# A new layout for the first three blocks of a convolution and MLP kernel: both token halves in both partition halves, W_in swapped by DMA

## The chip, the cores and the metric

The kernel runs on one core of a Trainium2 chip. The metric is device time in microseconds (us); a kernel is compared with another of the same rounds on the same chip. All times inside a kernel are counted from the start of its profiled span.

## The reference

A depthwise causal convolution with softmaxed weights (8 heads, 7 taps) over x of 8 x 4096 x 192, then an MLP with exact GELU:

```python
w = softmax(weight)                                  # 8 x 7
out[b, s, h, g] = sum_k w[h, k] * x_pad[b, s + k, h, g]
h = out.reshape(32768, 192) @ w_in                   # w_in 192 x 2048
g = 0.5 * h * (1 + erf(h / sqrt(2)))
result = g @ w_out                                   # w_out 2048 x 192
```

## The kernel before

The 32768 tokens are cut in two halves. Partitions 0 to 63 hold channels of the first half, partitions 64 to 127 the same channels of the second half; 192 channels make three pieces p. The tokens of a half are worked through in blocks: four of 256, then thirty of 512. For each block VectorE transposes x, the convolution is made (blocks 0 to 2 on TensorE with diagonal matrices, later ones on VectorE), mm1 multiplies by W_in, ACT applies GELU, and mm2 multiplies by W_out while mm1 of the next block runs.

Both partition halves need all of W_in. To save start-up traffic each half loads only one half of its columns, and TensorE copies the other half across:

```python
def dup(s):                                          # 4 pieces of 256 columns
    ...
    for p in range(NP):
        for hf in range(2):
            ins = t.matmul(DUPB[s][ro, p * FQ : (p + 1) * FQ], idb[r, :],
                           win[r, p * F + s * FQ : p * F + (s + 1) * FQ],
                           tile_position=(64 * hf, 64 - 64 * hf))
    ins.then_inc(S_DUP)

def pconv(n, p):                                     # blocks 0 to 2
    ...
    for k in range(KS - 1, -1, -1):
        for hf in range(2):
            ins = t.matmul(b[r, o : o + w], dg[r, d0 : d0 + 64], xTb[n][r, x0 : x0 + w],
                           start=(k == KS - 1), stop=(k == 0),
                           tile_position=(64 * hf, 64 * hf))
```

The loads. POOL issues W_in in two parts and then `wout` (W_out); SP issues the weight table, half of block 0's x, then, after the first part of W_in has landed, the rest, up to block 3; block 4 follows once block 1 has been transposed. ACT issues the other halves of blocks 0 and 1 at once.

```python
# POOL
win_in(0, FQ, S_WIN[0])
...                                                  # masks
win_in(FQ, FH, S_WIN[1])
g.dma_start(wout..., woutt...).then_inc(S_WOUT, 16)
for n in range(NB):
    halo(n)
# SP
load(sp, 0, (0, 1)); sp.wait_ge(S_WIN[0], 32)
load(sp, 1, (0, 1)); load(sp, 2); load(sp, 3)
for n in range(1, NB):
    if n + 3 < NB:
        load(sp, n + 3)                              # waits until the buffer is transposed
    store(sp, n - 1)
```

The first mm2 stands in block 1 and waits for `wout`:

```python
if n == 1 and i == i0:                               # i0 = 2
    t.wait_ge(S_WOUT, 16)
for un in todo[a0:a1]:
    mm2(n - 1, *un)
```

## Time and profile before

| | before |
|---|---|
| time, medians over the sessions | 700.4 to 702.2 us |
| span of the profiled run | 698.3 us |
| TensorE busy | 99% |
| first mm1 / first mm2 | 12.70 / 28.74 us |
| block 2 / block 5 starts on TensorE | 38.93 / 77.36 us |
| `wout` issued / landed | 5.66 / about 25.6 us |

From about 80 us on both kernels have the same rhythm, 0.66 us of mm1 and 0.66 us of mm2 in turn. A difference in time is therefore a difference in the start of block 5. The lines that carry this are shown in the prediction.

### The profile page before, as it was taken

The numbers are of one execution on the slowest core, as the hardware profiler recorded it, in microseconds if no ns is written. First come the engines' busy times: TensorE is split into PE (matmuls) and PEld (weight loads), VectorE is DVE, ScalarE is ACT, GpSimd is POOL, SyncE is SP. The second block draws the span as 40 slices with busy tenths as digits, with TensorE's granted clock in tenths as the row PEclk, the third lists the DMA queues.
The fourth block names the chain that finished last, engine by engine and source line by source line (L and its number), as shares of the span: only waits on it lengthen the run. The fifth ranks groups of instructions, "written<-read, shape, count | busy, mean of one in ns | idle before, by whom it ended". The sixth has DMA issues, their size and how long they took to land.

```text
span 698.3 us, 25401 instructions
## 1 busy us (share of the span) xinstructions
PE 689.0 (99%) x11625; PEld 528.7 (76%) x11625; DVE 551.5 (79%) x908; ACT 529.0 (76%) x524; POOL 39.5 (6%) x87
## 2 busy tenths in 40 slices
PE   8999999999999999999999999999999999999998
PEld 4797677777777777777777777777777777777777
DVE  3599978898888898888898888898888898888811
ACT  4577877777777777777777777777777777777771
POOL 4100000000000000000000000000000000000000
PEclk9999999999999999999999999999999999999999
DMA  9758533555533555533455533455533455521013
GB/s 202 157 131 194 125 75 86 120 136 137 121 88 84 119 136 138 121 86 87 118 137 137 121 93 82 116 137 136 129 87 82 114 137 136 124 60 24 24 48 92
DMA packets 22667, 78.15 MB, mean 112 GB/s; under 512 B 6945, under 2 KB 10785, under 8 KB 18721
## 3 DMA queue, kind: packets, MB, share of 16 engines
q1 hardware_dynamic: 18832, 73.80, 44.4%
q0 software_dynamic: 2896, 1.57, 1.6%
q8 instruction: 91, 1.49, 0.9%
q10 hardware_dynamic: 832, 1.16, 0.6%
q14 instruction: 16, 0.12, 0.1%
HBM read 52.92 MB, written 25.17 MB: 112 GB/s over the span
## 4 chain that ended last, share of the span: by engine, by line
PE 96%; DVE 3%; issue 1%; POOL 0%; ACT 0%; POOLq 0%; DVEq 0%
PE ob L650 48%; PE hp L616 46%; DVE acc L403 1%; PE ob L579 1%; PE hp L523 1%; DVE xT L373 0%; DVE xc L403 0%; DVE acc L396 0%; PE ob L529 0%; POOL win L229 0%; DVE osb L412 0%; ACT gT L509 0%; DVE win L344 0%; PE ob L551 0%; POOL sel L237 0%
## 5 line engine op out<-in xcount | busy, mean ns | idle before, releaser
L509 ACT ACTIVATE gT<-hp 128x1024 bf16<-128x1024 f32 x512 | 523.5, 1024 | 148.5 <-PE hp L616 148.5
L650 PEld LDWEIGHTS ob<-wout,gT 64*128 64x128 bf16 x8192 | 367.7, 94 | 100.0 <-PE ob L650 0.6
L650 PE MATMUL ob<-wout,gT 64*128 64x192 bf16 x8192 | 427.9, 243 | 0.1
L616 PE MATMUL hp<-xc,win 64*128 64x512 bf16 (+1 forms) x3264 | 422.9, 363 | 3.6 <-DVE xc L403 1.6
L403 DVE SCALAR_TENSOR_TENSOR acc<-xT,wcol,acc 128x512 f32<-128x512 f32 (+1 forms) x465 | 311.1, 733 | 0.0
L616 PEld LDWEIGHTS hp<-xc,win 64*128 64x128 bf16 x3264 | 165.0, 94 | 57.3 <-ACT gT L509 4.3
L412 DVE COPY osb<-ob 128x384 f32<-128x384 f32 x128 | 70.4, 550 | 125.1 <-PE ob L650 125.0
L403 DVE SCALAR_TENSOR_TENSOR xc<-xT,wcol,acc 128x512 bf16<-128x512 f32 (+1 forms) x93 | 63.4, 734 | 0.0
L373 DVE STREAM_TRANSPOSE xT<-xin 128x512 f32<-128x512 f32 (+1 forms) x102 | 61.2, 649 | 0.0
L396 DVE TENSOR_SCALAR acc<-xT,wcol 128x512 f32<-128x512 f32 (+1 forms) x93 | 54.1, 633 | 1.1
L302 POOL COPY xT<-xT 128x558 f32<-128x558 f32 x31 | 20.2, 652 | 590.1 <-DVE xT L373 590.1
L285 POOL COPY xT<-xT 128x18 f32<-128x18 f32 x28 | 11.1, 398 | 0.0
L579 PE MATMUL ob<-xTb,dg 64*64 64x256 bf16 x126 | 9.1, 291 | 0.3 <-DVE xTb L351 0.3
L579 PEld LDWEIGHTS ob<-xTb,dg 64*64 64x64 bf16 x126 | 6.8, 116 | 2.8 <-issue 1.1
L359 DVE CAST xc<-ob 128x256 bf16<-128x256 f32 x6 | 2.5, 422 | 6.8 <-PE ob L579 6.8
L523 PE MATMUL hp<-warm 128*128 128x512 bf16 x13 | 5.9, 629 | 1.3 <-DVE warm L313 1.3
L344 DVE CAST win<-ob 128x768 bf16<-128x768 f32 x3 | 2.9, 952 | 3.6 <-PE ob L551 3.6
L523 PEld LDWEIGHTS hp<-warm 128*128 128x128 bf16 x13 | 1.6, 137 | 3.8 <-issue 2.5
L296 POOL CAST xTb<-xT 128x186 bf16<-128x186 f32 x9 | 3.4, 384 | 14.6 <-DVE xT L373 14.6
L488 ACT ACTIVATE xc<-ob 128x256 bf16<-128x256 f32 x3 | 1.2, 384 | 3.2 <-PE ob L579 3.2
L344 DVE CAST win<-hp 128x768 bf16<-128x768 f32 x1 | 1.0, 958 | 3.2 <-PE hp L551 3.2
L480 ACT ACTIVATE xTb<-xT 128x256 bf16<-128x256 f32 x3 | 1.1, 417 | 2.8 <-DVE xT L373 2.8
(34 smaller groups left out, 21.4 us busy)
## 6 DMA issues: line engine op xcount, KB each, us to landing
xin<-in_x_dram SPq DMA_DIRECT2D x120, 380.0 KB, 6.7
out_dram<-osb SPq DMA_DIRECT2D x116, 192.0 KB, 3.1
xin<-in_x_dram SPq DMA_DIRECT2D x12, 188.0 KB, 7.3
out_dram<-osb SPq DMA_DIRECT2D x40, 48.0 KB, 1.8
wout<-in_moe_w_out_dram POOLq DMA_DIRECT2D x1, 768.0 KB, 19.9
xin<-in_x_dram ACTq DMA_DIRECT2D x4, 188.0 KB, 5.4
win<-in_moe_w_in_dram POOLq DMA_DIRECT2D x2, 288.0 KB, 6.3
out_dram<-osb ACTq DMA_DIRECT2D x8, 48.0 KB, 2.0
```

The costliest lines, as they stand in the source:

```text
L285: g.tensor_copy(dst, ap(xT[(n - 1) % 2], WS[n - 1] + 31, [[NP * XW, 128], [XW, NP], [32, HB]],),).then_inc(S_HALO)
L302: g.tensor_copy(ap(t, 1, [[NP * tw, 128], [tw, NP], [32, HB], [1, 31]]), ap(t, WS[n], [[NP * tw, 128], [tw, NP], [32, HB], [1, 31]]),).the ...
L344: v.tensor_copy(ap(win, FH + s * FQ, [[NP * F, 128], [F, NP], [1, FQ]]), ap(DUPB[s], 0, [[1024, 128], [FQ, NP], [1, FQ]]),).then_inc(S_DUPE)
L373: v.transpose(ap(xT[n % 2], p * XW + HL, [[NP * XW, 128], [1, w]]), ap(xin[n % NX], 64 * p, [[TB // 32 * D, 128], [D, w // 32], [1, 32]],) ...
L396: ins = v.tensor_scalar(a, src, wk, None, ALU.mult)
L403: ins = v.scalar_tensor_tensor(dst, src, wk, a, op0=ALU.mult, op1=ALU.add)
L412: v.tensor_copy(ap(osb[m % 2], g * C, [[8 * C, 128], [4 * C, 2], [1, C]]), ap(ob[(G0[m] + g) % 2], 0, [[1024, 128], [512, 2], [1, C]]),).t ...
L509: a.activation(out=ap(gT[n % 2], i * c * 2 * w, dst), in_=ap(hp[u % 2], 0, src), func=AF.Gelu,).then_inc(S_GELU)
L523: t.matmul(hp[1][:, 0:512], warm[:, 0:128], warm[:, :])
L579: ins = t.matmul(b[r, o : o + w], dg[r, d0 : d0 + 64], xTb[n][r, x0 : x0 + w], start=(k == KS - 1), stop=(k == 0), tile_position=(64 * hf, ...
L616: ins = t.matmul(hp[u % 2][:, hf * TB + cc * w : hf * TB + cc * w + w], win[r, p * F + wcols(hf, f0) : p * F + wcols(hf, f0) + 128], xc[n ...
L650: ins = t.matmul(ob[gg % 2][:, 512 * sub : 512 * sub + C], gT[m % 2][r, c0 : c0 + 128], wout[r, CH[i] * C : (CH[i] + 1) * C], start=(ph == ...
```

## The change

Its intent: in blocks 0 to 2 a 64-row partition half works only with the half of W_in that it holds, on the tokens of both halves. The convolution then has to deliver every token to both partition halves, which it does by using four 64x64 tiles per tap instead of two. No copying on TensorE and no casts on VectorE are needed; the other half of W_in comes later by a DMA inside SBUF, the swap, for block 3. The softmax is made on all 128 partitions, from a weight table broadcast at load. `wout` is issued later, so that block 1's x comes first.

```diff
-    wsb 8x7, sel 8 x 384, three fp32 matmuls to spread the weights ...
+    wsb 128 x 56, mask msk, softmax on 128 partitions ...
-            def dup(s): ... 4 x 6 matmuls, 4 casts on VectorE
 # convolution, blocks 0 to 2
-                        b[r, o : o + w], ... tile_position=(64 * hf, 64 * hf)
+                    for cf in range(2):
+                        CONVB[n][p][64 * cf : 64 * cf + 64, 512 * hf : 512 * hf + w], ...
+                        tile_position=(64 * hf, 64 * cf)
 # mm1, blocks 0 to 2
+                if n < ND:
+                    for p in range(NP):
+                        for hf in range(2):
+                            t.matmul(hp[u % 2][:, hf * TB : (hf + 1) * TB],
+                                     win[r, p * F + 128 * i : p * F + 128 * i + 128],
+                                     xc[n % 2][r, p * TB : (p + 1) * TB], ...)
 # POOL
-            win_in(FQ, FH, S_WIN[1]); wout issued here
+            win_in(FQ, 2 * FQ, S_WIN[1]); win_in(2 * FQ, FH, S_WIN[2])
+            halo(0)
+            g.wait_ge(S_XIN[1], 64)          # block 1's x has landed
+            wout issued here
 # ACT
+            a.wait_ge(S_WSB, 16)
             load(a, 0, (2, 3))
-            load(a, 1, (2, 3))
 # SP
-            load(sp, 1, (0, 1))
+            load(sp, 1)
             load(sp, 2)
             load(sp, 3)
+            for i in range(3): sp.wait_ge(S_WIN[i], 32)
+            for hf in range(2):
+                sp.dma_start(win of half hf, columns FH.., from win of half 1 - hf, columns 0..FH)
+                  .then_inc(S_WIN[3], 16)
 # VectorE: reads of mm2 results of block 0, position (block, instruction)
-            late = {(0, 0): (3, 4), (0, 1): (3, 14), ...
+            late = {(0, 0): (3, 10), (0, 1): (3, 18), ...
```
(cut: index arithmetic, the softmax instructions, the convolution taps spread between the mm1 units, PSUM buffers and semaphore counts)

More of the change, by code (lines that the diff above doesn't have):

```diff
@@ L62, in bass_lightweight_conv__then__act_gelu_exact_kernel @@
     G0 = [sum(NG[:n]) for n in range(NB + 1)]
-    CH = []
-    for s in range(4):
-        CH += [2 * s, 2 * s + 1, NF // 2 + 2 * s, NF // 2 + 2 * s + 1]
+    CH = [NF // 2 * h + i for i in range(NF // 2) for h in range(2)]
     PLAIN = [NCH[n] > 1 or n == NB - 1 for n in range(NB)]
@@ L91, in bass_lightweight_conv__then__act_gelu_exact_kernel @@
         wout = sbt("wout", [128, NF * C], BF16)
-        wsb = sbt("wsb", [H, KS], F32)
-        wmx = sbt("wmx", [H, 1], F32)
-        wsm = sbt("wsm", [H, 1], F32)
-        wrc = sbt("wrc", [H, 1], F32)
-        wex = sbt("wex", [H, KS], F32)
-        wnm = sbt("wnm", [H, KS], F32)
-        sel = sbt("sel", [H, NP * 128], F32)
+        wsb = sbt("wsb", [128, H * KS], F32)
+        wmx = sbt("wmx", [128, H], F32)
+        wsm = sbt("wsm", [128, H], F32)
+        wrc = sbt("wrc", [128, H], F32)
+        wex = sbt("wex", [128, H * KS], F32)
+        wnm = sbt("wnm", [128, H * KS], F32)
+        msk = sbt("msk", [128, NP * H], F32)
+        wpr = sbt("wpr", [128, NP * KS * H], F32)
         wcol = sbt("wcol", [128, NP * KS], F32)
@@ L114, in bass_lightweight_conv__then__act_gelu_exact_kernel @@
         S_WSB = sem("S_WSB")
-        S_WIN = [sem("S_WIN%d" % i) for i in range(2)]
+        S_WIN = [sem("S_WIN%d" % i) for i in range(4)]
         S_WOUT = sem("S_WOUT")
@@ L118, in bass_lightweight_conv__then__act_gelu_exact_kernel @@
         S_OUT = [sem("S_OUT%d" % i) for i in range(2)]
-        S_MSET = sem("S_MSET")
-        S_SEL = sem("S_SEL")
+        S_MSK = sem("S_MSK")
         S_IDN = sem("S_IDN")
-        S_PEP = sem("S_PEP")
         S_WARM = sem("S_WARM")
@@ L130, in bass_lightweight_conv__then__act_gelu_exact_kernel @@
         S_PCE = sem("S_PCE")
-        S_DUP = sem("S_DUP")
-        S_DUPE = sem("S_DUPE")
         S_HALO = sem("S_HALO")
@@ L142, in bass_lightweight_conv__then__act_gelu_exact_kernel, with pce @@
         block = es.enter_context(nc.Block())
-        DUPB = [hp[0], ob[1], ob[0], ob[1]]
-        CONVB = [
-            [(ob[0], 0), (ob[0], 512), (ob[1], 0)],
-            [(ob[0], 0), (ob[0], 512), (ob[1], 0)],
-            [(ob[1], 0), (ob[1], 512), (ob[1], 256)],
-        ]
+        CONVB = [[ob[0], ob[1], hp[1]], [ob[0], ob[1], ob[0]], [ob[1], ob[1], ob[1]]]
+        def pce(n, p):
+            return NP * n + p + 1 + (min(p + 1, NP) if n == 0 else NP)
         NCV = NP * KS
@@ L234, in _ @@
             win_in(0, FQ, S_WIN[0])
-            g.wait_ge(S_MSET, 2)
-            pat = [[64, NP], [0, 2], [1, 64]]
-            g.affine_select(
-                out=sel[:, :],
-                in_=sel[:, :],
-                compare_op=ALU.is_ge,
-                fill=0.0,
-                base=0,
-                pattern=pat,
-                channel_multiplier=-GRP,
-            ).then_inc(S_SEL)
-            g.wait_ge(S_SEL, 1)
-            g.affine_select(
-                out=sel[:, :],
-                in_=sel[:, :],
-                compare_op=ALU.is_ge,
-                fill=0.0,
-                base=GRP - 1,
-                pattern=[[-a, b] for a, b in pat],
-                channel_multiplier=GRP,
-            ).then_inc(S_SEL)
+            g.memset(msk[:, :], 1.0).then_inc(S_MSK)
+            g.memset(idb[:, :], 1.0).then_inc(S_MSK)
+            g.wait_ge(S_MSK, 2)
+            for hf in range(2):
+                m = msk[64 * hf : 64 * hf + 64, :]
+                g.affine_select(
+                    out=m,
+                    in_=m,
+                    compare_op=ALU.is_ge,
+                    fill=0.0,
+                    base=0,
+                    pattern=[[64, NP], [-GRP, H]],
+                    channel_multiplier=1,
+                ).then_inc(S_MSK)
+            g.wait_ge(S_MSK, 4)
+            for hf in range(2):
+                m = msk[64 * hf : 64 * hf + 64, :]
+                g.affine_select(
+                    out=m,
+                    in_=m,
+                    compare_op=ALU.is_ge,
+                    fill=0.0,
+                    base=GRP - 1,
+                    pattern=[[-64, NP], [GRP, H]],
+                    channel_multiplier=-1,
+                ).then_inc(S_MSK)
             for hf in range(2):
@@ L266, in _ @@
                 ).then_inc(S_IDN)
-            win_in(FQ, FH, S_WIN[1])
-            g.dma_start(
-                ap(wout, 0, [[NF * C, 128], [C, NF], [1, C]]),
-                ap(woutt, 0, [[C, 128], [128 * C, NF], [1, C]]),
-            ).then_inc(S_WOUT, 16)
+            win_in(FQ, 2 * FQ, S_WIN[1])
+            win_in(2 * FQ, FH, S_WIN[2])
             def halo(n):
@@ L278, in halo @@
                     g.wait_ge(S_CV, cvd(n - 2))
-                elif n >= 2:
-                    g.wait_ge(S_PCE, NP * (n - 1))
+                elif n >= ND:
+                    g.wait_ge(S_PCE, pce(n - 2, NP - 1))
                 if OFF[n] % SEQ == 0:
@@ L307, in _ @@
             g.wait_ge(S_IDN, 2)
-            for n in range(NB):
+            halo(0)
+            g.wait_ge(S_XIN[1], 64)
+            g.dma_start(
+                ap(wout, 0, [[NF * C, 128], [C, NF], [1, C]]),
+                ap(woutt, 0, [[C, 128], [128 * C, NF], [1, C]]),
+            ).then_inc(S_WOUT, 16)
+            for n in range(1, NB):
                 halo(n)
@@ L313, in _ @@
             v.memset(warm[:, :], 0.0).then_inc(S_WARM)
-            v.memset(sel[:, :], 1.0).then_inc(S_MSET)
-            v.memset(idb[:, :], 1.0).then_inc(S_MSET)
+            hk = [[H * KS, 128], [KS, H], [1, KS]]
             v.wait_ge(S_WSB, 16)
             v.tensor_reduce(
-                wmx[:, :], wsb[:, :], mybir.AxisListType.X, ALU.max, negate=True
+                wmx[:, :], ap(wsb, 0, hk), mybir.AxisListType.X, ALU.max, negate=True
+            ).then_inc(S_PRO)
+            v.wait_ge(S_PRO, 1)
+            v.tensor_tensor(
+                ap(wex, 0, hk), ap(wsb, 0, hk), ap(wmx, 0, [[H, 128], [1, H], [0, KS]]), ALU.add
             ).then_inc(S_PRO)
             v.wait_ge(S_ACTP, 2)
+            v.tensor_reduce(
+                wsm[:, :], ap(wnm, 0, hk), mybir.AxisListType.X, ALU.add
+            ).then_inc(S_PRO)
+            v.wait_ge(S_PRO, 3)
             v.tensor_scalar(wsm[:, :], wsm[:, :], 1e-9, None, ALU.add).then_inc(S_PRO)
-            v.wait_ge(S_PRO, 2)
+            v.wait_ge(S_PRO, 4)
             v.reciprocal(wrc[:, :], wsm[:, :]).then_inc(S_PRO)
-            v.wait_ge(S_PRO, 3)
-            v.tensor_scalar(
-                wnm[:, :], wex[:, :], wrc[:, 0:1], None, ALU.mult
+            v.wait_ge(S_PRO, 5)
+            v.tensor_tensor(
+                ap(wex, 0, hk), ap(wnm, 0, hk), ap(wrc, 0, [[H, 128], [1, H], [0, KS]]), ALU.mult
             ).then_inc(S_PRO)
-            v.wait_ge(S_PEP, 1)
-            v.tensor_copy(wcol[:, :], ob[0][:, 0 : NP * KS]).then_inc(S_PRO)
-            v.wait_ge(S_PRO, 5)
+            v.wait_ge(S_PRO, 6)
+            v.wait_ge(S_MSK, 6)
+            v.tensor_tensor(
+                ap(wpr, 0, [[NP * KS * H, 128], [KS * H, NP], [H, KS], [1, H]]),
+                ap(wex, 0, [[H * KS, 128], [0, NP], [1, KS], [KS, H]]),
+                ap(msk, 0, [[NP * H, 128], [H, NP], [0, KS], [1, H]]),
+                ALU.mult,
+            ).then_inc(S_PRO)
+            v.wait_ge(S_PRO, 7)
+            v.tensor_reduce(
+                wcol[:, :],
+                ap(wpr, 0, [[NP * KS * H, 128], [H, NP * KS], [1, H]]),
+                mybir.AxisListType.X,
+                ALU.add,
+            ).then_inc(S_PRO)
+            v.wait_ge(S_PRO, 8)
             v.wait_ge(S_IDN, 2)
@@ L339, in diag @@
                 ).then_inc(S_DG)
-            def dup_out(s):
-                v.wait_ge(S_DUP, s + 1)
-                v.tensor_copy(
-                    ap(win, FH + s * FQ, [[NP * F, 128], [F, NP], [1, FQ]]),
-                    ap(DUPB[s], 0, [[1024, 128], [FQ, NP], [1, FQ]]),
-                ).then_inc(S_DUPE)
             def cast(n, p):
@@ L357, in conv_out @@
                 v.wait_ge(S_PC, NP * n + p + 1)
-                b, o = CONVB[n][p]
+                hs = [1] if n == 0 else [0, 1]
                 v.tensor_copy(
-                    xc[n % 2][:, p * TB : p * TB + WS[n]], ap(b, o, [[1024, 128], [1, WS[n]]])
+                    ap(
+                        xc[n % 2],
+                        p * TB + 128 * hs[0],
+                        [[NP * TB, 128], [128, len(hs)], [256, 2], [1, 128]],
+                    ),
+                    ap(
+                        CONVB[n][p],
+                        512 * hs[0],
+                        [[1024, 128], [512, len(hs)], [128, 2], [1, 128]],
+                    ),
                 ).then_inc(S_PCE)
@@ L369, in trans @@
                     elif n >= 2:
-                        v.wait_ge(S_PCE, NP * (n - 1))
+                        v.wait_ge(S_PCE, pce(n - 2, NP - 1))
                     if n >= 1:
@@ L427, in _ @@
             diag(0)
-            diag(1)
             for p in range(NP):
                 trans(0, p)
+            diag(1)
             diag(2)
-            for q in range(3):
-                dup_out(q)
+            for p in range(NP):
+                conv_out(0, p)
             for n in range(1, ND):
@@ L438, in _ @@
                     cast(n, p)
-                if n == 1:
-                    dup_out(3)
-                for p in range(NP):
-                    conv_out(n, p)
-            late = {(0, 0): (3, 4), (0, 1): (3, 14), (1, 0): (4, 1), (1, 1): (4, 9)}
+                if n < ND - 1:
+                    for p in range(NP):
+                        conv_out(n, p)
+            late = {(0, 0): (3, 10), (0, 1): (3, 18), (1, 0): (4, 1), (1, 1): (4, 9)}
             late.update({(2, 0): (4, 16), (2, 1): (4, 23), (3, 0): (5, 14), (3, 1): (6, 1)})
@@ L455, in _ @@
                 for o, op in enumerate(ops0):
+                    if b == ND and o in (2, 5, 8):
+                        conv_out(ND - 1, o // 3)
                     while order and late[order[0]] <= (b, o):
@@ L465, in _ @@
             a.activation(out=hot[:, 0:1], in_=warm[0:1, 0:1], func=AF.Exp).then_inc(S_ACTP)
+            a.wait_ge(S_WSB, 16)
             load(a, 0, (2, 3))
             a.wait_ge(S_ACTP, 1)
-            a.wait_ge(S_PRO, 1)
-            a.activation(
-                out=wex[:, :],
-                in_=wsb[:, :],
-                func=AF.Exp,
-                bias=wmx[:, 0:1],
-                accum_out=wsm[:, 0:1],
-            ).then_inc(S_ACTP)
+            a.wait_ge(S_PRO, 2)
+            a.activation(out=wnm[:, :], in_=wex[:, :], func=AF.Exp).then_inc(S_ACTP)
             a.activation(out=hot[:, 1:2], in_=warm[0:1, 0:1], func=AF.Gelu).then_inc(S_HOT)
-            load(a, 1, (2, 3))
             for p in range(NP):
@@ L486, in _ @@
                 a.wait_ge(S_PC, p + 1)
-                b, o = CONVB[0][p]
                 a.activation(
-                    out=xc[0][:, p * TB : p * TB + WS[0]],
-                    in_=ap(b, o, [[1024, 128], [1, WS[0]]]),
+                    out=ap(xc[0], p * TB, [[NP * TB, 128], [256, 2], [1, 128]]),
+                    in_=ap(CONVB[0][p], 0, [[1024, 128], [128, 2], [1, 128]]),
                     func=AF.Copy,
@@ L500, in _ @@
                         a.wait_ge(S_MM2, G0[n - 1])
-                    if not PLAIN[n]:
+                    if n < ND:
+                        src = [[2 * TB, 128], [1, 2 * TB]]
+                        dst = [[NF * 2 * TB, 128], [1, 2 * TB]]
+                    elif not PLAIN[n]:
                         src = [[2 * TB, 128], [w // 4, 8], [32, w // 128], [1, 32]]
@@ L520, in _ @@
             t.wait_ge(S_WARM, 1)
-            def spin(k):
-                for i in range(k):
-                    t.matmul(hp[1][:, 0:512], warm[:, 0:128], warm[:, :])
-            spin(5)
-            t.wait_ge(S_SEL, 2)
-            t.wait_ge(S_PRO, 4)
-            for p in range(NP):
-                ins = t.matmul(
-                    ob[0][:, p * KS : (p + 1) * KS],
-                    sel[:, p * 128 : (p + 1) * 128],
-                    wnm[:, :],
-                )
-            ins.then_inc(S_PEP)
@@ L535, in _ @@
-            spin(8)
-            def dup(s):
-                if s == 0:
-                    t.wait_ge(S_IDN, 2)
-                    t.wait_ge(S_WIN[0], 32)
-                elif s == 1:
-                    t.wait_ge(S_WIN[1], 32)
-                    t.wait_ge(S_PCE, NP)
-                elif s == 3:
-                    t.wait_ge(S_DUPE, 2)
-                for p in range(NP):
-                    for hf in range(2):
-                        r = slice(64 * hf, 64 * hf + 64)
-                        ro = slice(64 - 64 * hf, 128 - 64 * hf)
-                        ins = t.matmul(
-                            DUPB[s][ro, p * FQ : (p + 1) * FQ],
-                            idb[r, :],
-                            win[r, p * F + s * FQ : p * F + (s + 1) * FQ],
-                            tile_position=(64 * hf, 64 - 64 * hf),
-                        )
-                ins.then_inc(S_DUP)
@@ L559, in pconv @@
-            def pconv(n, p):
-                w = WS[n]
-                b, o = CONVB[n][p]
-                t.wait_ge(S_CAST, NP * n + p + 1)
-                t.wait_ge(S_HALO, HC[n] + 2 + p)
-                if n == 0:
-                    t.wait_ge(S_DG, p + 1)
-                elif n == 1 and p == 0:
-                    t.wait_ge(S_DUPE, 3)
-                elif n == 1 and p == 2:
-                    t.wait_ge(S_DUPE, 4)
-                elif n == 2 and p == 0:
-                    t.wait_ge(S_PCE, 2 * NP)
-                elif n == 2 and p == 2:
-                    t.wait_ge(S_PCE, 2 * NP + 1)
-                for k in range(KS - 1, -1, -1):
-                    for hf in range(2):
-                        r = slice(64 * hf, 64 * hf + 64)
-                        d0 = (p * KS + k) * 64
-                        x0 = p * XB + 32 * k
-                        ins = t.matmul(
-                            b[r, o : o + w],
+            for i in range(16):
+                t.matmul(hp[0][:, 0:512], warm[:, 0:128], warm[:, :])
@@ new lines, in pconv @@
+            def pconv(n, p, k):
+                w = WS[n]
+                if k == KS - 1:
+                    t.wait_ge(S_CAST, NP * n + p + 1)
+                    if n == 0:
+                        t.wait_ge(S_DG, p + 1)
+                    elif n == 1 and p == 2:
+                        t.wait_ge(S_PCE, pce(1, 0))
+                    elif n == 2:
+                        t.wait_ge(S_PCE, pce(2, p) - 1)
+                if k == KS - 2:
+                    t.wait_ge(S_HALO, HC[n] + 2 + p)
+                for hf in range(2):
+                    r = slice(64 * hf, 64 * hf + 64)
+                    d0 = (p * KS + k) * 64
+                    x0 = p * XB + 32 * k
+                    for cf in range(2):
+                        ins = t.matmul(
+                            CONVB[n][p][64 * cf : 64 * cf + 64, 512 * hf : 512 * hf + w],
@@ L584, in pconv @@
                             stop=(k == 0),
-                            tile_position=(64 * hf, 64 * hf),
+                            tile_position=(64 * hf, 64 * cf),
                         )
-                ins.then_inc(S_PC)
-            pconv(0, 0)
-            pconv(0, 1)
-            dup(0)
-            pconv(0, 2)
-            behind = {(0, 1): [(dup, 1)], (0, 2): [(dup, 2)], (0, 3): [(dup, 3)]}
-            for p in range(NP):
-                behind[0, 4 + p] = [(pconv, 1, p)]
-                behind[1, 1 + p] = [(pconv, 2, p)]
+                if k == 0:
+                    ins.then_inc(S_PC)
+            taps = [(p, k) for p in range(NP) for k in range(KS - 1, -1, -1)]
+            for p, k in taps:
+                pconv(0, p, k)
+            behind = {}
+            for n, i0, i1 in ((1, 2, 7), (2, 1, 5)):
+                for i in range(i0, i1):
+                    j0 = len(taps) * (i - i0) // (i1 - i0)
+                    j1 = len(taps) * (i + 1 - i0) // (i1 - i0)
+                    behind[n - 1, i] = [(n, *q) for q in taps[j0:j1]]
             def mm1(n, i):
@@ L605, in mm1 @@
                     if n < ND:
-                        t.wait_ge(S_PCE, NP * (n + 1))
+                        t.wait_ge(S_PCE, pce(n, NP - 1))
                     else:
                         t.wait_ge(S_CV, cvd(n))
-                if n == 0 and i % 2 == 0:
-                    t.wait_ge(S_DUPE, i // 2 + 1)
-                for cc in range(c):
+                    if n == ND:
+                        t.wait_ge(S_WIN[3], 32)
+                if n == 0 and i in (0, 2, 4):
+                    t.wait_ge(S_WIN[i // 2], 32)
+                if n < ND:
+                    for p in range(NP):
+                        for hf in range(2):
+                            r = slice(64 * hf, 64 * hf + 64)
+                            ins = t.matmul(
+                                hp[u % 2][:, hf * TB : (hf + 1) * TB],
+                                win[r, p * F + 128 * i : p * F + 128 * i + 128],
+                                xc[n % 2][r, p * TB : (p + 1) * TB],
+                                start=(p == 0),
+                                stop=(p == NP - 1),
+                                tile_position=(64 * hf, 0),
+                            )
+                for cc in range(c if n >= ND else 0):
                     f0 = 128 * CH[i * c + cc]
@@ L635, in mm2 @@
                         elif gg == 1:
-                            t.wait_ge(S_PCE, NP * ND)
+                            t.wait_ge(S_PCE, pce(ND - 1, NP - 1))
                     else:
@@ L669, in _ @@
                     mm1(n, i)
-                    for f, *q in behind.get((n, i), []):
-                        f(*q)
+                    for q in behind.get((n, i), []):
+                        pconv(*q)
                     i0 = 2 if n == 1 else 0
@@ L688, in _ @@
         def _(sp):
-            sp.dma_start(wsb[:, :], ap(wt, 0, [[KS, H], [1, KS]])).then_inc(S_WSB, 16)
+            sp.dma_start(wsb[:, :], ap(wt, 0, [[0, 128], [1, H * KS]])).then_inc(S_WSB, 16)
             load(sp, 0, (0, 1))
             sp.wait_ge(S_WIN[0], 32)
-            load(sp, 1, (0, 1))
+            load(sp, 1)
             load(sp, 2)
             load(sp, 3)
+            for i in range(3):
+                sp.wait_ge(S_WIN[i], 32)
+            for hf in range(2):
+                sp.dma_start(
+                    ap(win, 64 * hf * NP * F + FH, [[NP * F, 64], [F, NP], [1, FH]]),
+                    ap(win, 64 * (1 - hf) * NP * F, [[NP * F, 64], [F, NP], [1, FH]]),
+                ).then_inc(S_WIN[3], 16)
             for n in range(1, NB):
```

## The prediction

> **What bounds the kernel now.** I read the page first, then the chain of waits of the first 60 us, then the chain from 55 to 85 us, then the DMA view cut into stretches, and last the view of the second weight, `wout`.
>
> The page says that TensorE has almost no idle time over the whole span:
>
> ```profile
> span 698.3 us, 25401 instructions
> PE 689.0 (99%) x11625; PEld 528.7 (76%) x11625; DVE 551.5 (79%) x908; ACT 529.0 (76%) x524; POOL 39.5 (6%) x87
> ```
>
> So the steady state belongs to TensorE, and the change does not touch it: only the first three blocks and the prologue differ. Everything is decided before about 80 us. The chain of waits there:
>
> ```profile
> 5.41 3.52 PE hp L523 x8
> 8.94 2.18 PE ob L579 x15
> ...
> 12.70 1.48 PE hp L616 x24
> 14.18 0.46 PE ob L551 x6
> 14.64 0.02 issue
> 14.67 0.97 DVE win L344
> ...
> 28.80 0.93 PE ob L650 x20
> ...
> 38.93 0.66 PE hp L616 x12
> ```
>
> Here L579 is the convolution on TensorE, L616 the first matrix product (mm1), L551/L344 the copying of W_in to the other half, and L650 the second product (mm2). The reader should take three marks: mm1 starts at 12.70, mm2 at 28.7, and block 2 starts at 38.7, after which mm1 and mm2 alternate at 0.66 us each. The chain from 55 to 85 us shows a second bound:
>
> ```profile
> 60.49 0.74 DVE xc L403
> 61.23 1.82 DVE xT L373 x3
> ...
> 75.80 1.42 DVE xc L403 x2
> 77.22 0.14 issue
> 77.36 0.82 PE hp L616 x6
> ```
>
> Blocks 4 and 5 start when VectorE has finished their convolution. A saving on TensorE therefore counts only as far as VectorE also gets to block 3 earlier. The mark that sets the end is 77.36, the start of block 5; from there on TensorE alone decides.
>
> The DMA engines are the third resource. They are busy from 2 to 29 us. The stretch 11 to 12.5 us holds `wout` alone, and 14 to 21 us holds `wout` (queue q0) beside the loads of x (q1):
>
> ```profile
> q0 software_dynamic: 750, 0.29, 159.2%
> ```
> ```profile
> q1 hardware_dynamic: 373, 1.49, 92.3%
> q0 software_dynamic: 371, 0.14, 16.4%
> ```
>
> Alone `wout` moves 500 packets per us (750 in 1.5); beside x it moves 53 (371 in 7), as many packets as x, but packets sixteen times smaller. The view of `wout` gives the consequence:
>
> ```profile
> L268 POOL DMA_DIRECT2D wout<-in_moe_w_out_dram x1: 1182/1182/1182, 5.7 to 5.7; - x1
> DMA to landing us min/median/max: 19.9/19.9/19.9
> ```
>
> Issued at 5.7, landed at about 25.6; mm2 needs it at 28.7. The slack is 3 us.
>
> **What the Trainium skill says.** (1) "DMA: Bandwidth & Descriptors", section on queues, rings and completion order: each DMA engine goes round the queues that have work, one packet at a time. The trace agrees: 371 against 373 packets in the same stretch. (2) "TensorEngine Tiling (Array Packing)", Tiling Modes: at 64x64 there are four independent tiles, and changing the mode drains the array. The trace agrees with the second: a convolution of 14 matmuls takes 0.95 us by the timeline, and its successor begins only 0.2 us after its last one was issued. No run here shows four tiles yet. (3) "TensorE: Matmul & The Clock Gate", Part 1: after an idle window of about 3.4 us the array clock halves, and a busy window brings it back. The trace agrees with the ramp: 11 pairs of 256-column matmuls take 2.25 us at 8.9 us (0.2 each), 7 pairs take 0.95 at 19.3 (0.14 each, tail included). (4) Same DMA page, issuing engines are not separate queues: all transfers share the same 16 engines, so the added swap competes with `wout`.
>
> **The change part by part.**
>
> Prologue. Softmax on 128 partitions avoids three fp32 matmuls (1.44 us at 3.97) and the read-back of `wcol`. The new VectorE chain has about eight small instructions of 0.15 to 0.3 us, and the weight table lands about 2.5 (2.2 before): `wcol` is ready at about 4.7, the first diagonal at 5.3, against 5.67 for its start before. But the transposes wait for x of block 0, which the first convolution needs anyway; with half its issues now behind the weight table I put it at 6.3. Transposes to 7.4, the other two diagonals to 8.6, halo casts on POOL to about 8.5. TensorE warms up without a break (16 matmuls instead of 5, 3 fp32 ones and 8), so the convolution should run at full clock: 21 taps. Before, a tap was two matmuls of 256 columns; now four, one per tile. If four tiles run together a tap still costs 0.11 us, so 2.3 us in all, ending about 10.1; copying out is split between ACT and VectorE, 0.4 us. mm1 starts at about 10.8: **1.9 us earlier** than 12.70.
>
> Blocks 0 and 1. Gone are 24 copying matmuls, in four groups of about 0.5 us, and four VectorE casts of 0.96 us, two of which stood on the chain. mm1 is 6 matmuls of 512 columns instead of 12 of 256: the same stream, 0.65 us. Six convolutions are spread over nine units: each has two mode switches of 0.11 us, as before. Block 1 needs its x. Before, ACT had issued half of it at 2.6; now SP issues all of it after the first part of W_in has landed (about 7.2). Landing about 13, transposes, then the `wout` issue on POOL (1.2 us) stands ahead of its halo: the first convolution tap of block 1 runs at about 15.1, so TensorE waits about 1.3 us after the third unit. Five units of 0.65 + 0.22 + 0.46 = 1.33 us bring the last but one unit of block 0 to about 20.9. Copies out of PSUM are now 512 columns (0.7 us estimated from 0.42 for 256) and block 2's three convolutions share one buffer and wait for them. TensorE reaches the first mm2 at about 26.5, **2.2 us before** 28.7. The VectorE chain into block 3 moves forward likewise.
>
> The transfer of `wout`. It is moved from 5.7 to after block 1's x has landed, about 13, data from about 15. I count rows by the access patterns: `wout` is 128x16 = 2048 rows of 384 B; x of a small block is 4x32 = 128 rows of 6 KB, of block 4 128 rows of 12 KB; the swap is 2x64x3 = 384 rows of 2 KB. Before, nearly half of `wout` moved while SP's loads had not begun to flow (8 to 12.7 us). Now, ahead of it or beside it on SP's queue, all issued without a gap by about 15.5: the rest of block 1 and block 2 (done at about 15), block 3 (0.77 MB at 0.21 MB/us, to 18.9), the swap (0.79 MB, to about 22.5), block 4 (1.56 MB at 0.2, to about 30). Packet for packet, `wout` gets 128 + 384 + 128 = 640 of its 2048 rows through by then. The other 1400 need 1400/500 = 2.8 us. It **lands at about 33**, 7.4 us later than before and 6.5 us after TensorE needs it.
>
> The path. mm2 starts at 33 instead of 28.7: +4.3. An idle stretch of 6.5 us lets the clock halve; while it does a full busy window at half speed loses 1.7 to 3.4 us, 2.6 taken. The work to block 2's start grows from 10 to about 11 us (two convolution pieces and two waits on the shared buffer): +0.7 with what overlaps. That is +7.6 at block 2. VectorE is held too, because block 2's second convolution stands on TensorE behind the waiting mm2. The 1.4 us that TensorE lost to VectorE at block 4 is recovered in part, since TensorE now comes late there itself: -1.5 or so. Sum: about **+6 us** at block 5 and so at the end: 702.2 + 6 = 708.
>
> **The rivals.** (a) `wout` lands in time, at 26 or earlier: there is a gap in SP's queue (before, such a gap at 21 to 22 us let through 284 packets in one slice of a microsecond), or the swap goes in smaller packets and so gives `wout` more turns. Then mm2 starts 2 us earlier, block 2 about 1 to 1.5 earlier, and VectorE, whose reads of block 3 also come earlier, sets block 5 at about 74.5 to 75: -2 to -3 us, 699.5. That is what the change intends. For it: someone set the positions with care. Against it: the one-for-one count above and a queue that has no reason to run dry. (b) Four tiles do not load together, and a tap costs 0.2 us: +2 us on each of three blocks, but with `wout` at 33 most of it lies in the shadow of that wait: 709 to 710. With rival (a) as well it gives 703. (c) The start is bound by the arrival of x of block 1 and not by TensorE; then the gain of the prologue is lost, 702 to 703 without a wait for `wout`.
>
> **Range and chances.** I give the late `wout` about 0.7, centred on 708, with 705 to 712 for the landing between 31 and 35 and the length of the cold stretch; in-time cases about 0.3, centred on 700, 697 to 703. Runs spread by 2.4 us. Point 707; eight times in ten between 698.5 and 711.5. 2% is 14 us, more than either mechanism gives: faster 0.01, same 0.97, slower 0.02.
>
> **What would show it.** Right: in the view of `wout`, a landing at 31 to 35 us; TensorE idle 5 to 8 us before the first mm2, and pairs twice as long after it; block 2 beginning at about 46; in a DMA stretch around 20 us equal packet counts on q0 and q1. mm1 beginning at 10 to 11.5; convolution taps at 0.11 us. Wrong: the first mm2 before 28.7 with no idle time ahead of it, a landing before 26, or VectorE still the releaser of blocks 4 and 5 at an earlier time than 77.

## The result, and the profile after

The changed kernel took 711.4 us (median of 4 runs, 709.4 to 712.3) against 701.3 (4 runs, 700.3 to 702.8): **1.4% slower**, ratio 1.0138 with a 95% interval of 1.0105 to 1.0171.

The head of the page of the changed kernel:

```profile
span 708.9 us, 25313 instructions
PE 689.8 (97%) x11580; PEld 522.2 (74%) x11580; DVE 552.0 (78%) x908; ACT 528.9 (75%) x523; POOL 41.0 (6%) x93
```

TensorE is busy for as long as before (689.8 against 689.0 us) but idle for 10 us more. The chain of waits of its first 60 us (start, length, what) says where:

```profile
8.75 6.82 DMA xin<-in_x_dram
15.56 0.29 issue
15.85 19.43 DMA wout<-in_moe_w_out_dram
35.28 0.04 issue
35.32 1.78 PE ob L652 x20
...
49.09 0.65 PE hp L605 x6
```

The chain that sets the end runs through the load of block 1's x, then for 19.4 us through the load of `wout`, and into the first mm2 at 35.32, 6.6 us later than before. Block 2 begins at 49.09, 10.2 us later. TensorE's waits of the first 95 us (in total, times, longest) and the stretch from 55 to 95 us of the chain:

```profile
PE ob L652 <- DMA wout<-in_moe_w_out_dram: 5.8, 1, 5.8
PE hp L618 <- DVE xc L429: 1.6, 2, 1.4
```
```profile
85.91 1.41 DVE xc L429 x2
87.32 0.14 issue
87.45 0.82 PE hp L618 x6
```

TensorE waits 5.8 us for `wout`, and then, as before, 1.6 us for VectorE at blocks 4 and 5. Block 5 begins at 87.45 instead of 77.36: of the 10.6 us between the two spans 10.1 are lost by then. Next, stretches of the same profile (from:to, length, busy time of TensorE, weight loads, VectorE, ACT, POOL, then the granted TensorE clock, DMA share, GB/s):

```profile
9.70:12.60 2.90, 2.90 (x56) 2.47 (x60) 1.81 (x4) 0.99 (x3) 0.91 (x2) 0.50 1.05 262
35.30:39.90 4.60, 4.06 (x42) 2.34 (x42) 0.47 (x1) 1.02 (x1) 0.00 (x0) 0.50 0.00 0
39.90:49.10 9.20, 8.70 (x162) 6.28 (x164) 6.38 (x16) 3.95 (x4) 0.41 (x1) 1.00 0.11 26
```

After the wait, TensorE works 4.6 us at half clock. It also worked at half clock from 9.7 to 12.6, for block 0's convolution. Last, the queues (packets, MB, share) between 24 and 28 us, and between 16 and 23 us:

```profile
q1 hardware_dynamic: 115, 0.89, 95.6%
q0 software_dynamic: 113, 0.04, 8.9%
```
```profile
q1 hardware_dynamic: 615, 1.70, 102.1%
q0 software_dynamic: 44, 0.02, 1.9%
```

Beside block 4's x, `wout` (q0) gets one small packet for each large one: 0.04 MB of its 0.79 in 4 us. In the 7 us before, it got almost nothing: its issue at 15.85 found blocks 2 and 3 and the swap already queued, and its first packets moved only after 22 us (run 7 comes back to this).

### The profile page after: what moved, and what is told of

It is laid out like the page before. It is cut to its first block, busy times and chain, and to the rows that moved or that the text cites. A ratio compares the mean times of both kernels' runs of the same rounds, so it can differ in the third digit from the quotient of the medians.

```text
span 708.9 us, 25313 instructions
## 1 busy us (share of the span) xinstructions
PE 689.8 (97%) x11580; PEld 522.2 (74%) x11580; DVE 552.0 (78%) x908; ACT 528.9 (75%) x523; POOL 41.0 (6%) x93
## 4 chain that ended last, share of the span: by engine, by line
PE 90%; DMA 4%; DVE 4%; issue 1%; SPq 0%; POOL 0%; DVEq 0%; POOLq 0%
PE ob L652 46%; PE hp L618 42%; DMA wout<-in_moe_w_out_dram 3%; DVE acc L429 3%; DMA xin<-in_x_dram 1%; PE hp L605 1%; DMA win<-in_moe_w_in_dram 1%; DVE xc L429 1%; DVE xT L399 0%; DVE acc L422 0%; PE ob L565 0%; DVE osb L438 0%; SPq L170 0%; POOL win L224 0%; DVE xc L376 0%
## 5 line engine op out<-in xcount | busy, mean ns | idle before, releaser
L652 PEld LDWEIGHTS ob<-wout,gT 64*128 64x128 bf16 x8192 | 369.0, 94 | 107.7 <-DMA wout<-in_moe_w_out_dram 6.1
L652 PE MATMUL ob<-wout,gT 64*128 64x192 bf16 x8192 | 429.1, 243 | 6.0 <-DMA wout<-in_moe_w_out_dram 5.8
L618 PE MATMUL hp<-xc,win 64*128 64x512 bf16 (+1 forms) x2976 | 403.8, 373 | 1.6 <-DVE xc L429 1.6
L618 PEld LDWEIGHTS hp<-xc,win 64*128 64x128 bf16 x2976 | 152.6, 94 | 51.7 <-ACT gT L532 2.0
L605 PE MATMUL hp<-xc,win 64*128 64x512 bf16 x144 | 20.1, 388 | 1.3 <-ACT gT L532 0.6
L376 DVE CAST xc<-ob 128x512 bf16<-128x512 f32 (+1 forms) x8 | 5.0, 625 | 18.4 <-PE ob L565 18.4
L565 PE MATMUL ob<-xTb,dg 64*64 64x256 bf16 x224 | 10.5, 319 | 4.9 <-ACT xTb L501 2.6
L565 PEld LDWEIGHTS ob<-xTb,dg 64*64 64x64 bf16 x224 | 6.5, 124 | 11.0 <-issue 5.8
L605 PEld LDWEIGHTS hp<-xc,win 64*128 64x128 bf16 x144 | 6.2, 96 | 7.5 <-ACT gT L532 2.4
L224 POOL DMA_DIRECT2D win<-in_moe_w_in_dram x6 | 3.9, 655 | 0.8 <-POOLq L725 0.8
## 6 DMA issues: line engine op xcount, KB each, us to landing
wout<-in_moe_w_out_dram POOLq DMA_DIRECT2D x1, 768.0 KB, 19.4
```

The source lines that it names most:

```text
L565: ins = t.matmul(CONVB[n][p][64 * cf : 64 * cf + 64, 512 * hf : 512 * hf + w], dg[r, d0 : d0 + 64], xTb[n][r, x0 : x0 + w], start=(k == KS ...
L605: ins = t.matmul(hp[u % 2][:, hf * TB : (hf + 1) * TB], win[r, p * F + 128 * i : p * F + 128 * i + 128], xc[n % 2][r, p * TB : (p + 1) * T ...
L618: ins = t.matmul(hp[u % 2][:, hf * TB + cc * w : hf * TB + cc * w + w], win[r, p * F + wcols(hf, f0) : p * F + wcols(hf, f0) + 128], xc[n ...
L652: ins = t.matmul(ob[gg % 2][:, 512 * sub : 512 * sub + C], gT[m % 2][r, c0 : c0 + 128], wout[r, CH[i] * C : (CH[i] + 1) * C], start=(ph == ...
```

## The experiments

Theory 1: the time is lost because `wout` lands late, and it lands late because SP's queue beside it is full (blocks 2 and 3, swap, block 4). Theory 2, the rival: the new prologue costs it; mm1 begins at 14.12 instead of 12.70, because the broadcast weight table lands at 4.05 (VectorE's first use; 2.23 before) and ACT's loads of x wait for it. Within theory 1 there is a second question: is it the late issue of `wout` or the traffic beside it?

**1. `wout` issued early.**

```diff
             win_in(2 * FQ, FH, S_WIN[2])
+            wout issued here
             halo(0)
-            g.wait_ge(S_XIN[1], 64)
-            wout issued here
```

> The changed kernel with the load of wout issued where the kernel before had it, right behind the loads of W_in, not after the x of block 1. Theory 1 (the late landing of wout costs the time, by holding up mm2 and VectorE's block 3): wout lands at 26 to 31 us instead of 35.3, the first mm2 runs at 30 to 31, no wait of over 1 us on wout, and the time falls from 711.4 to 702 to 706. It also delays the x of block 1 by up to 3 us, so not all of the 10 us come back. Theory 2 (the prologue costs it: the weight table lands at 4.0 and mm1 begins at 14.1 instead of 12.7): the time stays at 710 to 712 or grows.

Measured: 710.5 us, ratio to the kernel before 1.0138. The expected landing was missed. `wout`, issued 8.8 us earlier, landed only one microsecond earlier, at 34.2:

```profile
L270 POOL DMA_DIRECT2D wout<-in_moe_w_out_dram x1: 1182/1182/1182, 7.1 to 7.1; - x1
DMA to landing us min/median/max: 27.2/27.2/27.2
```

From 16 to 22 us of this run q1 moved 441 packets and q0 443. So the one-for-one turns hold, and the time of issue alone is not the cause.

**2. The swap and block 4's x wait for `wout`.**

```diff
             for i in range(3): sp.wait_ge(S_WIN[i], 32)
+            sp.wait_ge(S_WOUT, 16)
             for hf in range(2):  # swap
```

> The changed kernel with wout issued as it has it, but SP waits for the landing of wout before it issues the swap of W_in and the x of block 4, so that only x of blocks 2 and 3 stand beside wout. Theory 1, and within it the account that wout is slow because SP's queue is full of swap and block 4: wout lands at 24 to 26 us, the first mm2 at 29.5 without waiting, block 2 at 40 to 41 instead of 49.1, block 5 at 79 to 80, the time 702.5 to 704.5. If instead the late issue alone (15.85 against 5.66 us) makes it late, wout still lands after 30 us and the time stays above 707. Theory 2 expects 710 to 712.

Measured: 702.5 us, ratio 1.0025 (1.0008 to 1.0042). `wout` was issued at 15.98, as late as in the changed kernel, and landed at 26.2. Its view, then the chain of waits:

```profile
DMA to landing us min/median/max: 10.2/10.2/10.2
```
```profile
29.09 0.52 PE ob L565 x12
29.61 0.93 PE ob L652 x20
```

The first mm2 (L652) follows the convolution (L565) without a wait and at full clock. Block 2 began at 41.5, a little after the expected 40 to 41. One line on SP brings back about 8 of the 10 us, with the prologue left as it is. For these 8 us this decides between the theories, and between issue and traffic; the other 2 it leaves open.

**3. TensorE kept busy during the wait.**

```diff
+            for _ in range(28):
+                t.matmul(ob[0][:, 0:512], warm[:, 0:128], warm[:, :])
             t.wait_ge(S_WOUT, 16)
```

> The changed kernel with 28 idle-time matmuls on TensorE (into the PSUM buffer that mm2 is about to overwrite, about 6 us) ahead of the wait for wout, so that the array clock does not fall. wout lands as late as before. If the slow clock after the wait costs what I put on it, the first 20 mm2 take 0.9 instead of 1.78 us and the time falls by 1 to 2.5 us, to 709 to 710.5. If it is hidden by VectorE, the time stays within 0.5 us of 711.4.

Measured: 708.7 us, ratio 1.0113 against 1.0138 for run 1 and the changed kernel. `wout` landed at 35.7, and the first 20 mm2 took 1.0 us instead of 1.78:

```profile
35.66 0.05 issue
35.70 1.00 PE ob L652 x20
```

From the first mm2 to block 2 it took 11.9 us (35.70 to 47.62) instead of 13.8 (35.32 to 49.09). The half clock costs about 1.9 us here, and it reaches the end: 708.7 us, just under the expected 709 to 710.5, against 710.5 for run 1 in the same rounds.

**4. The kernel before with `wout` late, and nothing else of the change.**

```diff
-            wout issued here
-            for n in range(NB):
+            halo(0)
+            g.wait_ge(S_XIN[1], 64)
+            wout issued here
+            for n in range(1, NB):
                 halo(n)
```

> The kernel before with one part of the change alone: wout issued by POOL after its first halo and the landing of the x of block 1 (15.9 us). Theory 1: wout lands at 30 to 33 us instead of 25.6, because x of blocks 2, 3 and 4 stand beside it, mm2 starts 2 to 4 us later than 28.7, and the time grows by 2 to 5 us, to 703.5 to 706. Less than the 10 us of the whole change, because the swap is not in the queue. Theory 2: 701.3, unchanged.

Measured: 702.8 us, ratio 1.0031 (1.0016 to 1.0046). The chain of waits:

```profile
13.90 16.50 DMA wout<-in_moe_w_out_dram
30.40 0.04 issue
30.45 1.00 PE ob L652 x20
```

Landing at 30.4 instead of 25.6, first mm2 1.7 us later than before, about 2 us in time, at the low end of what was expected. The late issue does cost when it gives up the stretch in which `wout` had the engines alone; without the swap it costs a fifth of the whole.

**5. ACT's half of block 0's x issued at once, in the changed kernel.**

```diff
-            a.wait_ge(S_WSB, 16)
             load(a, 0, (2, 3))
```

> The changed kernel with ACT issuing its half of the x of block 0 at once, as the kernel before does, not after the weight table has landed (4.0 us). If the prologue is hidden by the wait for wout (theory 1): mm1 begins at 11 to 12.5 us instead of 14.1, wout still lands at 34 to 36, and the time stays at 710 to 712. If the late start of mm1 is what costs (theory 2): 707.5 to 709.

Measured: 711.2 us, ratio 1.0134. mm1 began at 12.2 instead of 14.1, `wout` landed at 34.7, and the time did not move. The prologue lies behind the wait for `wout`; theory 2 falls for the changed kernel.

**6. The same edit, on top of run 2.**

> The kernel of the run with the swap after wout (702.5), and ACT's half of the x of block 0 issued at once. wout is out of the way there, so the prologue can show. If block 1's first convolution is bound by the arrival of its x (15.7 us in that run), an earlier mm1 at 11 to 12.5 buys nothing: mm2 again at 29 to 29.6, time 701.8 to 702.8. If the start of mm1 sets the rest: mm2 at 27.5, time 700 to 701.

Measured: 704.5 us, ratio 1.0033 (1.0012 to 1.0054), not told apart from run 2 (1.0025). mm1 began at 12.15, but the first mm2 at 31.3, later than in run 2 (29.6). TensorE waited 2.5 us for VectorE's cast of block 1's x, and the clock records show half clock from 18.5 to 21.9 us. As expected nothing was gained; that the first mm2 came later was not expected, and the time missed the expected 701.8 to 702.8.

**7. The swap moved behind the first stores, block 4's x left in place.**

```diff
             load(sp, 3)
-            (waits and swap)
             for n in range(1, NB):
                 ...
                 store(sp, n - 1)
+                if n == 1: (waits and swap)
```

> The changed kernel with the swap of W_in moved behind the first stores on SP (about 45 us), so that block 4's x follows block 3's directly and the swap is not in the queue beside wout. This parts the swap from block 4's x. If the swap is the larger part of what delays wout: wout lands at 27 to 30 us, mm2 waits under 1 us, 702.5 to 703.5. If block 4's x alone is enough to starve it (12 KB packets one for one): wout at 31 to 34, 705 to 709. If the swap's own landing for block 3 becomes late (needed at about 52), the time grows instead; it should land by 50 to 58.

Measured: 707.8 us, ratio 1.0095. `wout` landed at 31.4:

```profile
DMA to landing us min/median/max: 15.6/15.6/15.6
```

The three landings divide the delay: 26.2 with neither beside it (run 2), 31.4 with block 4's x, 35.3 with the swap as well. Added in this order, block 4's x costs 5.2 us and the swap 3.9; the swap without block 4's x was not tried. Part of the delay comes before any turn is taken: the first packet of `wout` moved 2.3 us after its issue in run 2, 4.4 us in this run and 6.4 us in the changed kernel. POOL's program is the same in all three, so this too grows with what SP has queued; how is not shown.

**8. Three mendings together.** Run 2, run 5, and block 1's x issued by SP without waiting for W_in:

```diff
-            sp.wait_ge(S_WIN[0], 32)
             load(sp, 1)
+            sp.wait_ge(S_WIN[0], 32)
             load(sp, 2)
```

> A version meant to beat both: swap after wout has landed, ACT's half of block 0's x at once, and SP issues block 1's x without waiting for the first part of W_in. Expected: x of block 1 lands at 9 to 12 us instead of 15.6, wout is issued at 10 to 12 and lands at 20 to 25, mm1 begins at 11 to 12.5, the first mm2 runs at 26 to 28 without waiting, block 2 begins at about 38.5 to 40, time 698.5 to 701. If W_in's first part, no longer protected, lands after 11.5 us, mm1 begins later and half of that is lost.

Measured: 702.5 us, ratio 1.0018 (0.9996 to 1.0040), a miss of 1.5 us. Block 1's x landed at 11.9, and mm2 began at 28.6, no later than before. But mm1 began only at 13.76, at half clock (11.0 to 14.5 us), and from the first mm2 to block 2 it took 12.4 us (28.65 to 41.06), against 10.2 in the kernel before.

**9. More matmuls on zeros at the start (26 instead of 16), on top of run 8.**

> The version with all three mendings (702.5 us), with 26 instead of 16 matmuls on zeros at the start, so that TensorE is busy until the first convolution. In that version it idled from 7.1 to 9.65 us and the clock records show half clock from 11.0 to 14.5 us. If that half clock costs: block 0's convolution takes 2.5 us instead of about 3.6, mm1 begins at 12.2 to 12.7 instead of 13.76, first mm2 at 27 to 27.5. In the time: 700.8 to 701.8 if TensorE sets block 2, 702 to 703 if VectorE's reads of mm2 results set blocks 4 and 5 all the same.

Measured: 701.7 us, ratio 1.0022 (1.0007 to 1.0037), no better than run 8. The half clock is gone, mm1 begins at 12.8 and mm2 at 27.3, 1.4 us before the kernel before. Still block 5 begins at 78.05, released by VectorE. An earlier start of mm2 is not enough.

**10. Meeting points of VectorE and TensorE moved, on top of run 9.**

```diff
-        CONVB ... [ob[1], ob[1], ob[1]]]                  # block 2's convolution results
+        CONVB ... [ob[1], ob[0], ob[1]]]
-            ((1, 2, 7), (2, 1, 5))                        # units between which taps are put
+            ((1, 2, 7), (2, 1, 3))
-            (0, 0): (3, 10), (0, 1): (3, 18), (1, 0): (4, 1), (1, 1): (4, 9), (2, 0): (4, 16), (2, 1): (4, 23)
+            (0, 0): (3, 14), (0, 1): (4, 0), (1, 0): (4, 8), (1, 1): (4, 15), (2, 0): (4, 23), (2, 1): (5, 5)
-                    if b == ND and o in (2, 5, 8):        # VectorE reads block 2's results
+                    if b == ND and o in (2, 4, 7):
```
(with the semaphore waits that belong to them)

> The version with more matmuls at the start, and the meeting points of VectorE and TensorE moved: block 2's convolution is finished before the first mm2 and its three results alternate between two PSUM buffers, and VectorE reads out the mm2 results of blocks 0 to 2 later among its instructions, so that it does not wait for mm2. If the joint schedule and not the start alone holds the mended kernel at the level of the kernel before: block 2 begins at 38.5 to 39.5 instead of 41.5, VectorE waits under 1 us in all for mm2 before block 5, block 5 begins at 75.5 to 77 (77.4 in the kernel before), time 698.5 to 700.5, that is 0.1 to 0.4% faster than before. If blocks 4 and 5 are bound by VectorE's own work, 700.5 to 702.

Measured: **697.0 us** (6 runs), ratio 0.9957 (0.9939 to 0.9975), **0.4% faster than the kernel before**. TensorE no longer waits for VectorE at blocks 4 and 5. VectorE's waits from 30 to 95 us are now these, and in the same stretch no wait of TensorE is left:

```profile
DVE osb L438 <- PE ob L651: 5.5, 4, 3.6
DVE xc L429 <- PE hp L604: 0.7, 1, 0.7
```

Three parts of the expectation were missed, on the good side in time: 698.5 to 700.5 us was expected, block 2 at 38.5 to 39.5 (it began at 37.09, against 39.23 in run 9), and a wait of VectorE for mm2 of under 1 us. That wait is 5.5 us, longer than in any other run (1.3 to 3.2 us in this stretch). So the gain does not come from sparing VectorE this wait, as the edit was meant to; gone is its wait of 3.5 us for block 2's convolution (run 9, same stretch). The longer wait costs nothing because VectorE is still ahead: its convolution for block 5 is done at 73.1 us, and TensorE begins block 5 at 73.55. Which of the joined edits carries the 0.65% between runs 9 and 10 was not tried one by one.

**11. Later read-outs in the kernel before.** Positions (3, 10), (3, 20), (4, 5), (4, 12) instead of (3, 4), (3, 14), (4, 1), (4, 9), nothing of the change.

> The kernel before with VectorE's read-outs of the mm2 results of blocks 0 and 1 placed later among its instructions, and nothing of the change. In the kernel before, VectorE waits 1.3 us for mm2 and TensorE then waits 1.6 us for VectorE at blocks 4 and 5. If the gain of the best version lies in the joint schedule and not in the changed layout: 698.5 to 699.8, that is 0.1 to 0.3% faster. If the kernel before has nothing to gain from it: within 0.5 us of the kernel before, and block 5 again at 77.4.

Measured: 700.7 us, ratio 0.9990 (0.9974 to 1.0007): the same. The profiled run was its slowest (703.9): there `wout` happened to land at 31.0 and mm2 waited 2 us for it. So the margin of `wout` is thin in the kernel before too, as this one execution shows. The time met the second of the two expectations; block 5 at 77.4 cannot be checked in this disturbed profile (81.28). This run shows that later read-outs alone do not give what run 10 gave.

## Why the prediction was right, and where its sizes were off

The mechanism held: the late `wout` sets the start of mm2, the clock falls in the wait, VectorE is held up with it, and the prologue does not matter. The size did not hold: the sum for a late `wout` was +6 us, and +10.1 was measured. The point, 707, was 4.4 us short, and that 711.4 still lies in the range, 0.1 us under its upper end of 711.5, is luck. By its steps:

- **Landing of `wout`.** Predicted 33, measured 35.3. The base was early: block 1's x landed at 15.56, not 13. And "data from about 15" was wrong: it got practically no packet until 22. Both errors made it later, but only by 2 us, because block 4's x went through nearly when predicted and `wout` then ran alone: by 30 us 418 of its rows had moved (44 packets from 16 to 23 us, 374 from 23 to 30) instead of 640, and the last 1630 took 5.3 us instead of 2.8. One for one afterwards was right (113 to 115). But the prediction took all of x's packets for rows: in its stretch from 14 to 21 us 496 packets are under 512 B and only 371 of them are `wout`'s, so 125 of the 373 packets of x are small ones. To judge by the equal counts they take turns like the rows, and the count of 640 left them out. The split that the prediction implied, with both swap and block 4 at work, is shown by run 7.
- **TensorE ready for mm2.** Predicted 26.5, measured 29.5 (29.48 by the timeline, with the last convolution tap). The start of mm1, predicted 10.8, came at 14.12. The terms: the weight table 4.05 instead of 2.5, which moved block 0's x from 6.3 to about 8.75; the convolution at half clock after an idle stretch that was not foreseen ("TensorE warms up without a break" failed: it idled from 7.1 to 9.7). The kernel before was no faster at this point: its first 11 taps took 0.2 us each as well. A third term shows in run 5, where the first two are gone and mm1 still begins at 12.20: the softmax on VectorE, put at an end of 4.7, ends at about 7.5 there and in the changed kernel. None of it reached the end in the changed kernel (run 5). Whether it would have, had `wout` been in time, is not shown: run 2 is 0.25% slower than the kernel before, but an earlier mm1 on top of it gained nothing (run 6). In run 2 the chain of waits runs through block 1's x (landed at 15.7) and POOL's issue of `wout` to the convolution, as rival (c) had it, and its 702.5 is in that rival's range.
- **Four tiles per tap.** Right. Block 0's last convolution, 28 matmuls of 256 columns, took 0.93 us at full clock; seven taps at 0.11 and a tail. Rival (b) is refuted by this line of the timeline:

```profile
12.65 0.93 PE L565 MATMUL hp<-xTb,dg 64*64 64x256 bf16 x28
```

- **Half clock.** Predicted 2.6, measured about 1.9 (run 3).
- **The longer stretch to block 2.** Put at +0.7; without the half clock run 3 shows 11.9 us against 10.2 before, so +1.7. Block 2's convolutions in one buffer and their 512-column reads are the likely cause: the chain shows one such read (0.70 us at 39.43). How the rest divides is not shown.
- **"The 1.4 us that TensorE lost to VectorE at block 4 is recovered in part": failed.** TensorE waits for VectorE 1.6 us in both kernels, since VectorE was held up by the same wait (up to 9.1 us for one of block 2's convolution results). The -1.5 in the sum was 0.

With the measured terms: +6.6 (start of mm2), +1.9 (clock) and +1.7 (longer stretch) make +10.2 at block 2, which is what the chain shows, and nothing is given back.

## What to carry to other kernels

When a transfer is moved or put off, count the packets that stand in the other queues at its new place, not only the bytes: a transfer of small rows got its turns one for one with rows sixteen or thirty times larger, and issuing it earlier did not help while they were there. Let a bulk transfer with slack wait for a small-row transfer without slack; one wait on the issuing engine gave back 8 of 10 us. When two engines hand work to each other, an earlier start of one pays only after the meeting points have moved too.

## What the Trainium skill lacked or had wrong

- "DMA: Bandwidth & Descriptors", queues, rings and completion order: it describes round robin by packets of typically 9 to 17 descriptors, and does not say what this means for queues whose rows differ in size. Here the queues moved equal numbers of the profile's packets, 384 B of `wout` against up to 6 KB or 12 KB (443 to 441 and 113 to 115), so a queue of small rows got 4% of the bytes moved beside 12 KB rows. Whether a turn is one row or several is not shown.
- The same page, latency table: it gives a first byte of about 1 us for transfers issued from POOL. `wout`, issued at 15.85 with other transfers queued before it, moved its first packets after 22 us: about 6 us, and 2.3 us with less queued (run 2). The page does not say how much already queued work goes ahead.
- "TensorE: Matmul & The Clock Gate", Part 1: it asks for an idle window of about 3.4 us before the clock falls. Here an idle stretch of 2.6 us (7.1 to 9.7) was enough: the clock record falls at 9.2, 2.1 us after the last matmul. In the wait for `wout` it fell 3.6 us after (29.5 to 33.1).
- "TensorEngine Tiling (Array Packing)": no figure, on this page or another, for 64x64 tiles with a new weight for every matmul. Four at a time cost 0.11 us per tap of 256 columns, the same as two.
- No page: what a load costs that broadcasts one row of 224 B to 128 partitions. Here it landed at about 4.0 us, issued at 0.8, against about 2.2 for the 8 x 7 table, and at 4.9 in run 5 with ACT's x beside it.
